# Order of the weight-form and tap transfers in the first step of a convolution and feed-forward kernel

## The chip, the cores and the metric

The kernel runs on one core of a Trainium2 chip. The metric is device time in microseconds, from a few timed runs of the whole program; lower is better. The trace comes from one more execution under the hardware profiler. Its span runs from the first to the last instruction of the program.

The engines are named as in the profile: PE (matrix products; PEld is its weight load), DVE (vector), ACT (scalar activation), POOL (general purpose; it also issues DMAs with accumulation), SP (issues DMAs). Each engine works through its own instructions in order. Transfers issued by POOL go to DMA queue q0, those by SP to q1; both run on the same 16 DMA engines.

## The reference

The input x is 8 x 4096 x 192. A causal convolution over 7 positions comes first, whose 7 weights (a softmax per head, 8 heads of 24 columns) are shared by the columns of a head. The result goes through a feed-forward block with 2048 hidden columns and a sigmoid form of gelu:

```python
w = softmax(weight)                         # 8 heads x 7 taps
out[b, s, h, :] = sum(w[h, k] * x_pad[b, s + k, h, :] for k in range(7))
h = out.reshape(32768, 192) @ w_in          # 192 -> 2048
g = h * (1.0 / (1.0 + np.exp(-1.702 * h)))
y = g @ w_out                               # 2048 -> 192
```

## The kernel before, in words

**Steps.** The 32768 tokens are worked through in 32 steps (`big` 0 to 31 in the code), each of 512 positions of two batch entries. In each step the convolution yields blocks C11 to C32 (two by three blocks: 192 columns in three parts, c = 0, 1, 2), the first product (L614) yields the hidden columns, ACT applies gelu, and the second product (L989) yields the output. Both products use a scheme with fewer block products and more additions: V1 to V8 are sums of convolution blocks (`SUMS_C`, L159), of which V1 = C31 - C11 comes first, and 21 terms (`TERMS`, L206) make one of the two halves (v = 0, 1) of the first product. The second product needs sums of the output weights, the *weight forms* (25 of them, in `w_out_s` and `w_form`).

**Step 0 is special.** It uses plain products, because weights and sums are still being made: `first_step` (L1096) and, for its second product, the generator `second_first` (L763). Its second product is done by `go` (L817; lines L820 and L825 in the profile). Beside it run the preparation of step 1's and step 2's convolutions and the making of the weight forms.

**Weight forms.** `add_forms(stage)` (L430) makes a form by a copy on ACT (L433 or L435) and one or two accumulating transfers on POOL's queue (L437), in four stages. Stage 3 has four transfers, called F1 to F4 here: (23 += 0), (24 += 3), (1 += 22) and (7 += 21), 192 KB each. Afterwards `end_forms` (L439; L441 in the profile) negates forms 9, 17, 20 and 21 on ACT. Form 21 is read by F4, so its negation waits until F4 has landed. `end_forms` stands in the list `todo`, behind the preparation of step 2, and is reached in the second half (v = 1) of step 1's first product.

**Taps.** The convolution of a later step is made part by part. For c = 1, DVE multiplies and adds (L504). For c = 0 and 2, ACT multiplies x by each of the seven weights (`tap`, L512; L516 in the profile) and writes the product to a spare place, its home. For c = 0 the seven products are added by six accumulating transfers on POOL's queue (`TREE`, L509; L530 in the profile), 256 KB each. For step 2 they are called T1 to T6 here: T1 adds home 2 to home 1, T2 home 4 to 3, T3 home 6 to 5, T4 home 1 to the result, T5 home 5 to 3, T6 home 3 to the result. So T5 needs T2 and T3, and T6 needs T4 and T5. For c = 2, POOL itself adds each home to the result (L518), six additions. After these POOL makes V1 and the other sums (`sums_c`, L532; L393 and L391 in the profile). SP then copies V1 across the two halves of the partitions (`cross`, L539; L541 in the profile).

**What sets the order.** The order on each engine is that of the calls in the code, as no scheduler moves them. `ready` holds step 2's fourteen taps (c = 0, then c = 2); each `next_tap()` (L1052) issues one. In `second_first` nine of them are issued (L879 to L888), the others in `hidden` by `taps_at` (L669) in step 1. Transfers of a tree that are due are put in the list `tree`, and `end_taps(left)` (L527) issues them down to `left`. In step 2, `end_taps(2)` at the seventh tap of c = 0 leaves T5 and T6 in the list; the next tap, the first of c = 2, calls `end_taps(0)` and issues them. Only then does `first_step` call `add_forms(3)` (L1227), and then `end_taps()` (L1228) and the x load for step 3 (L1229).

**Where PE needs step 2.** In the second half of step 1's first product (`hidden`, L662, v = 1), PE does term 7, term 12, terms 5 and 17, then, once ACT has copied a bank (`copy2(k15, ...)`, L651 in the profile), term 0 and 13 more terms; then `fetch` (L1241) begins step 2's first product with term 16, which reads V1 and its copy across; then come terms 3 and 19.

Of the kernel before, what the change touches and what calls it, by code (L numbers as in the profile page):

```python
# [15 lines left out]
def kernel(  # L16
# [32 lines left out]
    H, K = weight.shape  # L49
# [126 lines left out]
    def own(big):  # L176
        return conv_t[:, big % 2 * 2, :, :]
# [41 lines left out]
    def form(i):  # L219

        if i < WHOLE:
            return w_out_s[:, i // NG, i % NG * NG : (i % NG + 1) * NG, :]
        return w_form[:, i - WHOLE, :, :]
# [206 lines left out]
    def add_forms(stage):  # L430
        for dst, src, *sign in COPY_O[stage]:
            if sign:
                act.mul(form(dst), form(src), -1.0)  # L433
            else:
                act.copy(form(dst), form(src))  # L435
        for dst, src in SUMS_O[stage]:
            nc.gpsimd.dma_start(out=form(dst), in_=form(src), accum_op=ALU.add)  # L437
# [49 lines left out]
    def tap_home(big, c, k):  # L487
        if big == 1:
            return homes_1[c][k - 1]
        if big < 3:  # L490
            return (first_taps if c == 0 else taps[3])[k - 1]
        return taps[c][k - 1]

    def conv_src(big, c, k, ns=slice(0, 2)):
        return xts[big][:, c, ns, Q - PAD + k : Q - PAD + k + T]

    def conv(big, c, k, ns=slice(0, 2), times=vec.tensor_scalar_mul):
        src = conv_src(big, c, k, ns)
        dst = own(big)[:, 2 * c + ns.start : 2 * c + ns.stop, :]
        tap = cw[:, c, k : k + 1]  # L500
        if k == 0:
            times(dst, src, tap)
        else:
            vec.scalar_tensor_tensor(  # L504
                out=dst, in0=src, scalar=tap, in1=dst, op0=ALU.mult, op1=ALU.add
            )
# [5 lines left out]
    def tap(big, c, k):  # L512

        dst = own(big)[:, 2 * c : 2 * c + 2, :]
        home = tap_home(big, c, k) if k else dst
        act.mul(home, conv_src(big, c, k), cw[:, c, k : k + 1])  # L516
        if k and c not in DMA_TAPS and big > 1:
            nc.gpsimd.tensor_add(dst, dst, home)  # L518
            return
        homes = [dst] + [tap_home(big, c, i) for i in range(1, K)]  # L520
        for a, b in (PAIRS_1 if big == 1 and c == 0 else TREE).get(k, ()):
            tree.append((homes[a], homes[b]))
        end_taps(2 if big == 2 and k == K - 1 else 0)

    tree = []

    def end_taps(left=0):  # L527
        while len(tree) > left:
            out, src = tree.pop(0)
            nc.gpsimd.dma_start(out=out, in_=src, accum_op=ALU.add)  # L530
# [71 lines left out]
    def prepare_taps(big):  # L602

        for c in (0, 2):
            for k in range(K):
                yield "", 1.0, lambda c=c, k=k: tap(big, c, k)
        yield f"taps {big}", 0.0, lambda: None
# [155 lines left out]
    def second_first(between, fetch, last_taps):  # L763
# [53 lines left out]
        def go(bank, steps, first=True, more=False):  # L817
            for i, (w, t) in enumerate(steps):
                for c in range(NC):
                    nc.tensor.matmul(  # L820
                        chunk(bank, c), w[:, chunk_cols(c)], t,
                        start=first and i == 0, stop=not more and i == len(steps) - 1, skip_group_check=True,
                    )
                dst, w, t, start, to = side.pop(0)
                nc.tensor.matmul(dst, w, t, start=start, stop=to is not False, skip_group_check=True)  # L825
                if to is not False:
                    act.copy(to, dst)
# [17 lines left out]
            (listed(s1, t1, (0,)), None, True), (listed(s1, t1, (1,)), p5, False), (p3[:6], q12, False),  # L845
        )
        last_taps()
        sub(t1[1], b12[1], b11[1])
        add(s1[1], a21[1], a22[1])
        go(a, listed(a11, b11))  # L850
# [1 line left out]
        sub(t2[1], b22[1], t1[1])  # L852
        for i in range(2):
            sub(s2[i], s1[i], a11[i])
        add_forms(0)
        need("first 1")
        go(c11, p2[:6], more=True)
        add_forms(1)
# [23 lines left out]
        for i in range(0, len(steps), 2):  # L882
            go(c21, steps[i : i + 2], first=False)
            if i in (0, 2):
                act.copy(sums[i // 2], slots[2][i // 2])
            next_tap()
            if i < 6:
                next_tap()  # L888
        assert not side
        turn(0, 0, blocks(p1), js)  # L890
# [161 lines left out]
    def next_tap():  # L1052
        if ready:
            ready.pop(0)[2]()
            while ready and ready[0][1] == 0:
                ready.pop(0)[2]()

    def need(label):
        for q in (todo, ready):
            while any(item[0] == label for item in q):  # L1060
                q.pop(0)[2]()
# [34 lines left out]
    def first_step(fetch):  # L1096
# [99 lines left out]
        def between():  # L1196
# [4 lines left out]
            ready.extend(prepare_taps(2))  # L1201

        rest = second_first(between, fetch, lambda: taps_next(len(taps_1)))

        def stage(n, todo=lambda: next(rest)):
# [88 lines left out]
```

## Time and profile before

| What | us |
|---|---|
| timed runs, median of three | 2286.95 |
| timed runs, lowest and highest | 2285.14, 2287.42 |
| the profiled execution's own time | 2284.85 |
| its span | 2282.9 |
| ACT busy | 1563.2 |
| POOL busy | 847.4 |

The profile's times count from the start of the span. A row of the timeline gives the start, the length, engine, line, operation and shape, how many instructions were merged, and in brackets how long the engine stood idle before and what ended that. A row of the chain of work gives start, length and what the time was spent on; "DMA a<-b" is a transfer from its issue to its landing. The granted clock is the share of its full speed that PE's clock was allowed.

### The profile page before, as it was taken

The page shows a single profiled execution, that of the slowest core. Times are in us where ns is not written, and L with a number is a line of the kernel's source. Part 1 is how long each engine was busy: PE and PEld are TensorE (multiplying, and loading weights), DVE is VectorE, ACT ScalarE, POOL GpSimd, SP SyncE. Part 2 cuts the span into 40 slices and gives each one's busy share as a digit, 9 for nine tenths or more (in the row PEclk, how much of TensorE's full clock was granted, in tenths as well). Part 3 has the DMA queues.
Part 4 walks back from the last instruction along what each step waited for, and adds up shares of the span by engine and source line. Part 5 has one row for each costly group of instructions (what it writes and reads, how often), then busy time and mean ns, then how long its engine had stood idle before and what let it go on. Part 6 is the DMA issues. An engine that isn't in the chain of part 4 may idle for free.

```text
span 2282.9 us, 60959 instructions
## 1 busy us (share of the span) xinstructions
PE 2266.0 (99%) x25214; PEld 1202.3 (53%) x25214; DVE 1934.6 (85%) x2794; ACT 1563.2 (68%) x2968; POOL 847.4 (37%) x834
## 2 busy tenths in 40 slices
PE   9989999999999999999999999999999999999999
PEld 4355555555555555555555555555555555555556
DVE  8878888888888888888888888888888888888877
ACT  8657766667766677666776667776667766667754
POOL 1444442343433444324434234443244442344400
PEclk9999999999999999999999999999999999999999
DMA  9966566575666665665656666556756566574443
GB/s 205 165 133 135 114 127 129 122 142 109 117 126 139 127 126 112 128 134 123 137 115 120 126 130 136 118 111 124 143 121 135 112 128 130 123 141 84 91 98 71
DMA packets 270228, 285.78 MB, mean 125 GB/s; under 512 B 118016, under 2 KB 206080, under 8 KB 269824
## 3 DMA queue, kind: packets, MB, share of 16 engines
q0 software_dynamic: 57648, 150.69, 36.8%
q1 hardware_dynamic: 210656, 130.80, 25.6%
q8 instruction: 199, 3.26, 0.6%
q14 instruction: 77, 0.63, 0.1%
q10 hardware_dynamic: 1648, 0.39, 0.1%
HBM read 53.15 MB, written 25.17 MB: 34 GB/s over the span
## 4 chain that ended last, share of the span: by engine, by line
PE 94%; DVE 2%; DMA 2%; ACT 1%; issue 0%; POOL 0%; SPq 0%; DVEq 0%; POOLq 0%; ACTq 0%
PE slot L614 33%; PE slot L989 33%; PE sums L614 15%; PE sums L989 12%; DMA g<-g 1%; DMA w_form<-w_form 0%; DMA conv_t<-conv_t 0%; DVE xt L473 0%; DMA w_out_s<-w_form 0%; DVE g L832 0%; DVE conv_t L504 0%; DVE w_in_s L391 0%; DMA xin<-in_x_dram 0%; DVE w_in_s L393 0%; DVE w_out_s L376 0%
## 5 line engine op out<-in xcount | busy, mean ns | idle before, releaser
L614 PE MATMUL slot<-conv_t,w_in_s 64*128 64x512 f32 x3740 | 862.1, 592 | 8.9 <-ACT room L651 8.6
L989 PE MATMUL slot<-g,w_form 128*32 128x256 f32 x7024 | 710.3, 379 | 0.0
L614 PEld LDWEIGHTS slot<-conv_t,w_in_s 64*128 64x128 f32 x3740 | 374.8, 187 | 435.7 <-issue 352.4
L393 DVE TENSOR_TENSOR g<-g 128x1024 f32<-128x1024 f32 x372 | 448.1, 1232 | 4.1 <-ACT g L640 0.8
L989 PEld LDWEIGHTS slot<-g,w_form 128*32 128x32 f32 x7024 | 373.5, 110 | 119.7
L614 PE MATMUL sums<-conv_t,w_in_s 64*128 64x512 f32 x1660 | 408.5, 591 | 0.3 <-DVE w_in_s L376 0.3
L640 ACT ACTIVATE g<-room 128x1024 f32<-128x1024 f32 x310 | 325.8, 1077 | 68.1 <-DVE room L655 66.3
L1014 ACT COPY room<-slot 32x256 f32<-32x256 f32 x434 | 159.2, 367 | 310.4 <-PE slot L989 309.3
L989 PE MATMUL sums<-g,w_form 128*32 128x256 f32 x2648 | 368.8, 379 | 0.0
L989 PE MATMUL slot<-g,w_out_s 128*32 128x256 f32 x4080 | 318.8, 380 | 0.0
L965 POOL DMA_DIRECT2D g<-g x124 | 106.3, 857 | 502.5 <-PE slot L989 157.3
L614 PEld LDWEIGHTS sums<-conv_t,w_in_s 64*128 64x128 f32 x1660 | 172.0, 187 | 187.8 <-issue 142.6
L518 POOL TENSOR_TENSOR conv_t<-conv_t,g 128x512 f32<-128x512 f32 x180 | 260.6, 1448 | 15.6 <-POOL conv_t L518 3.3
L530 POOL DMA_DIRECT2D g<-g x120 | 104.7, 890 | 424.4 <-PE sums L989 128.7
L651 ACT COPY room<-slot 128x512 f32<-128x512 f32 x434 | 231.5, 601 | 41.4 <-PE slot L614 41.4
L516 ACT ACTIVATE g<-xt,cw 128x512 f32<-128x512 f32 x360 | 248.5, 730 | 2.2
L989 PEld LDWEIGHTS slot<-g,w_out_s 128*32 128x32 f32 x4080 | 164.7, 110 | 131.7 <-ACT g L636 22.7
L636 ACT ACTIVATE g<-slot 128x512 f32<-128x512 f32 x334 | 180.8, 598 | 45.2 <-PE slot L614 25.1
L989 PEld LDWEIGHTS sums<-g,w_form 128*32 128x32 f32 x2648 | 177.9, 110 | 36.7
L504 DVE SCALAR_TENSOR_TENSOR conv_t<-xt,cw,conv_t 128x512 f32<-128x512 f32 (+1 forms) x198 | 187.9, 949 | 4.6
L393 POOL TENSOR_TENSOR conv_t<-conv_t 128x256 f32<-128x256 f32 x180 | 185.7, 1046 | 9.4
L1014 ACT COPY room<-sums 32x256 f32<-32x256 f32 x217 | 79.6, 367 | 144.2 <-PE sums L989 142.5
(204 smaller groups left out, 2899.0 us busy)
## 6 DMA issues: line engine op xcount, KB each, us to landing
g<-g POOLq DMA_DIRECT2D x124, 512.0 KB, 5.6
xin<-in_x_dram SPq DMA_DIRECT2D x240, 180.0 KB, 4.4
conv_t<-conv_t SPq DMA_DIRECT2D x180, 192.0 KB, 3.2
g<-g POOLq DMA_DIRECT2D x120, 256.0 KB, 3.7
out_dram<-osbs SPq DMA_DIRECT2D x186, 128.0 KB, 4.9
g<-room POOLq DMA_DIRECT2D x31, 512.0 KB, 5.3
conv_t<-g POOLq DMA_DIRECT2D x60, 256.0 KB, 4.7
g<-osbs POOLq DMA_DIRECT2D x30, 512.0 KB, 4.6
```

Source lines behind the costliest of these rows:

```text
L393: eng.tensor_sub(v(dst), v(a), v(b))
L504: vec.scalar_tensor_tensor(out=dst, in0=src, scalar=tap, in1=dst, op0=ALU.mult, op1=ALU.add)
L516: act.mul(home, conv_src(big, c, k), cw[:, c, k : k + 1])
L518: nc.gpsimd.tensor_add(dst, dst, home)
L530: nc.gpsimd.dma_start(out=out, in_=src, accum_op=ALU.add)
L614: nc.tensor.matmul(slot[h], w_in_s[halves[h], a, v * P : (v + 1) * P], src, start=first, stop=True, skip_group_check=True,)
L636: act.activation(dst[:, :, h, :], src[h].rearrange("p (o t) -> p o t", o=2), AF.Gelu_apprx_sigmoid)
L640: act.activation(dst.rearrange("p o h t -> p h o t"), src.rearrange("p h (o t) -> p h o t", o=2), AF.Gelu_apprx_sigmoid,)
L651: act.copy(bank(dst, h), bank(src, h))
L965: nc.gpsimd.dma_start(out=spot(dst), in_=spot(a), accum_op=ALU.add)
L989: nc.tensor.matmul(dst, w, t, start=first, stop=last, skip_group_check=True)
L1014: act.copy(to, d)
```

## The change

Three places are edited. `end_taps` leaves two transfers in the list at every tap of step 2's part c = 2 too (and at the last of c = 0), so T5 and T6 are issued by the `end_taps()` behind `add_forms(3)`. `second_first` issues eight of step 2's taps instead of nine; the ninth goes to the next place in `hidden` that takes a tap, and each later tap moves on by one. `add_forms(0)`, the first eight form copies on ACT with their six transfers on POOL, stands ahead of the first product `go(a, listed(a11, b11))` and so ahead of the copy `act.copy(p1, whole(a))` on ACT.

```diff
@@ tap
-        end_taps(2 if big == 2 and k == K - 1 else 0)
+        end_taps(2 if big == 2 and (c or k == K - 1) else 0)
@@ second_first
         last_taps()
+        add_forms(0)
         sub(t1[1], b12[1], b11[1])
         add(s1[1], a21[1], a22[1])
         go(a, listed(a11, b11))
         act.copy(p1, whole(a))
         sub(t2[1], b22[1], t1[1])
         for i in range(2):
             sub(s2[i], s1[i], a11[i])
-        add_forms(0)
         need("first 1")
@@ second_first, last loop
             next_tap()
-            if i < 6:
+            if i < 4:
                 next_tap()
```

On each engine this gives: PE, DVE and SP keep their order (on DVE only line numbers differ). On ACT the eight copies (L433, L435) come ahead of the product's copy (L851 before), and the taps shift as told. On POOL, T5 and T6 (L530) come behind F1 to F4 (L437), and all six additions of c = 2 (L518) follow T6; before, the first of the six stood between T6 and F1.

## The prediction

> **What bounds the kernel now.** I read the page first, then the waits of PE over the whole span, then the chain of work that ended last around the one long wait, then that stretch window by window.
>
> ```profile
> span 2282.9 us, 60959 instructions
> PE 2266.0 (99%) x25214; PEld 1202.3 (53%) x25214; DVE 1934.6 (85%) x2794; ACT 1563.2 (68%) x2968; POOL 847.4 (37%) x834
> PE slot L614 <- ACT room L651: 8.6, 1, 8.6
> ```
>
> PE is busy 2266.0 of 2282.9 us, so all its idle time is 16.9 us, and one single wait of 8.6 us holds half of it. The profiled execution took 2284.85 us: its span and 1.95 us around it. The three timed runs have a median of 2286.95, 2.1 us above it; I work out a difference on the profiled execution and apply it to the median. No edit touches steps 3 to 31, so all that can change lies around that wait. The chain there:
>
> ```profile
> 107.28 6.97 DMA g<-g
> ...
> 118.42 5.38 DMA w_out_s<-w_form
> ...
> 123.88 0.52 ACT w_form L441
> ...
> 124.93 2.56 PE slot L614 x4
> ```
>
> Read upwards: PE restarts at 124.93 because ACT copies its bank only then; ACT stands in end_forms (L441), which may negate form 21 only when the last form transfer, F4, has landed, at 118.42 + 5.38 = 123.80; F4 was issued late because POOL, which issues in order, stood before tap transfer T6 until T5 had landed, at 107.28 + 6.97 = 114.25. The wait began at 124.93 - 8.6 = 116.3. The clock adds to it (columns: window, length, busy times, then granted clock, DMA share, GB/s):
>
> ```profile
> 118.00:120.00 2.00, 0.00 (x0) 0.00 (x0) 0.00 (x0) 0.00 (x0) 2.00 (x5) 1.00 0.92 142
> 120.00:122.00 2.00, 0.00 (x0) 0.00 (x0) 0.00 (x0) 0.00 (x0) 2.00 (x2) 0.58 1.11 178
> ...
> 130.00:132.00 2.00, 2.00 (x11) 1.70 (x9) 0.33 (x1) 0.56 (x2) 1.92 (x3) 0.86 0.29 70
> ```
>
> A mean of 0.58 over 120 to 122 is a clock that falls to one half at 120.3, 4 us into the wait; 0.86 over 130 to 132 is one that is whole again at 130.56. From 124.93 on PE thus works 5.6 us at half speed, a loss of 2.8. So the wait costs 8.6 + 2.8 = 11.4 us, and that is all this change can reach.
>
> **Edit 1: T5 and T6 behind F1 to F4.** POOL's queue before, and behind it SP's first cross transfers:
>
> ```profile
> 95.62 3.98 POOL L530 DMA_DIRECT2D g<-g  x3
> 101.66 1.19 POOL L530 DMA_DIRECT2D conv_t<-g  x1 [2.06 <-PE sums L614]
> 107.28 1.19 POOL L530 DMA_DIRECT2D g<-g  x1 [4.43 <-DMA g<-g]
> 114.78 1.19 POOL L530 DMA_DIRECT2D conv_t<-g  x1 [6.32 <-PE slot L614]
> 115.53 1.74 POOL L518 TENSOR_TENSOR conv_t<-conv_t,g 128x512 f32<-128x512 f32 x1
> 116.74 2.28 POOL L437 DMA_DIRECT2D w_form<-w_out_s  x2
> ...
> 118.99 8.46 POOL L518 TENSOR_TENSOR conv_t<-conv_t,g 128x512 f32<-128x512 f32 x5
> 127.53 3.38 POOL L393 TENSOR_TENSOR conv_t<-conv_t 128x256 f32<-128x256 f32 x2
> 129.15 1.11 SPq L541 DMA_DIRECT2D conv_t<-conv_t  x2
> conv_t<-conv_t SPq DMA_DIRECT2D x2, 64.0 KB, 2.0
> ```
>
> Rows one to four are T1 to T3, T4, T5, T6. After the edit the order is T1 to T4, F1 to F4, T5, T6, then six L518 additions. F1 to F4 wait for their ACT copies (four of 0.43 to 0.5 us behind the tap at 94.22 that edit 2 shows, so done by 97) and for landed sums, so POOL issues them from about 102.2, right behind T4, in place of 116.7. That is 14 us earlier, but not landed 14 us earlier, since the transfers are bound by the DMA engines (rows: queue, packets, MB, share of the 16 engines; windows 104:108, 110.3:123.8 and 118:124), and the x loads for step 3 stand in SP's queue just then:
>
> ```profile
> q0 software_dynamic: 415, 0.41, 69.3%
> q1 hardware_dynamic: 1149, 0.28, 40.9%
> ...
> q0 software_dynamic: 1084, 1.27, 62.0%
> q1 hardware_dynamic: 1970, 1.19, 47.6%
> ...
> q0 software_dynamic: 676, 0.87, 91.9%
> 103.61 8.81 SPq L99 DMA_DIRECT2D xin<-in_x_dram  x8
> ```
>
> T4 landed at about 110.3 (the ACT row below waits for it until 110.40). From there to 123.80 the engines moved T5, T6 and F1 to F4 (1.27 MB) and the x loads (1.19 MB) with shares of together 109%: 13.5 us without a hole worth naming. With POOL's queue alone it is 0.87 MB in 5.8 us, 0.15 MB/us. The same work is left after the edit; only the order changes. F1 to F4 are 4 x 192 KB = 0.79 MB, T5 0.26 MB.
> - Bound from above: all x loads are served first, and only T6's 0.26 MB are left: 0.26 / 0.15 = 1.7 us. T5 lands at 123.8 - 1.7 = 122.1 and F4 1.7 ahead of it, at 120.4.
> - Bound from below: POOL's queue gets 69.3 of 110.2 parts, 63%, as in 104:108. F4 lands 0.79 / 0.15 / 0.63 = 8.4 us after 110.3, at 118.7, T5 0.26 / 0.15 / 0.63 = 2.8 later, at 121.5. At 0.18 MB/us (the 0.36 MB that the queue moved in 120:122, its fullest window) these are 117.3 and 119.6.
>
> I take about the middle: **F4 at 118.8, T5 at 121.0**. PE restarts 1.13 us after F4 (124.93 - 123.80), at 119.9 in place of 124.93: 5.0 us won, and the wait is then 3.6 us.
>
> What is late next: T6, the six additions (L518), V1 = C31 - C11 (the first L393) and its cross over SP (L541) all stand behind T5 on POOL. PE needs V1 when fetch begins step 2's first product. In the trace:
>
> ```profile
> 138.97 3.59 PE L614 MATMUL slot<-conv_t,w_in_s 64*128 64x512 f32 x15
> 186.40 9.03 POOL L518 TENSOR_TENSOR conv_t<-conv_t,g 128x512 f32<-128x512 f32 x6
> 195.51 0.73 POOL L393 TENSOR_TENSOR conv_t<-conv_t 128x256 f32<-128x256 f32 x1
> ```
>
> The first row gives 0.86 us for the four matmuls of a term (15 in 3.59, the last one 0.59 long). Its first four are term 18, so fetch began at 138.97 + 0.86 = 139.83: 14 terms (12.0) and the 2.8 of slow clock after the restart. V1 was ready at 129.15 + 0.5 + 2.0 = 131.7 (the second SP cross goes out 0.5 after the first, and the last row of POOL's fence has 2.0 to landing): 8 us early. After the edit it is T5's landing, 0.53 to T6's issue (114.78 - 114.25), 0.75 to the first addition (115.53 - 114.78), the six additions, V1, and 2.6 for the cross. The additions: 9.03, as step 3's six (second row), beside a busy DVE. V1: 0.73 there, 1.6 in 127.53's row (two in 3.38); I take 1.1. Sum 14.0. **V1 is ready at 121.0 + 14.0 = 135.0**; PE, on a clock that has not fallen, comes to fetch at 119.9 + 12.0 = 131.9 and waits 3.1 us. Fetch begins at 135.0 in place of 139.83: **4.8 us won**, not 11.4. With the ends of T5 (119.6, 122.1) and of the tail (13.6, 14.5) it is 133.2 to 136.6, a gain of 3.2 to 6.6.
>
> This sum hardly depends on the first wait's clock. If the clock does fall there, PE comes to fetch 2.8 later, at 134.7, still ahead of V1. The Trainium skill, in "TensorE: Matmul & The Clock Gate", section "Part 1: The HAM clock gate", says that a whole idle window of about 3.4 us halves the clock, that the windows run freely, and that one busy window restores it. The trace agrees as far as it goes: half speed about 4 us into the wait. By that rule either new wait can fall on a whole window or miss it.
>
> **Edit 2: one tap fewer in step 0.** The ACT rows:
>
> ```profile
> 94.22 0.72 ACT L516 ACTIVATE g<-xt,cw 128x512 f32<-128x512 f32 x1
> ...
> 110.40 1.06 ACT L640 ACTIVATE g<-room 128x1024 f32<-128x1024 f32 x1 [1.78 <-DMA conv_t<-g]
> ...
> 123.88 0.52 ACT L441 ACTIVATE w_form<-w_form 128x384 f32<-128x384 f32 x1 [8.26 <-DMA w_out_s<-w_form]
> ```
>
> The tap at 94.22 leaves, so the copies of F1 to F4 end 0.63 earlier; POOL reaches them only at 102.2, so that is worth nothing. Every later tap of step 2 slides one place, and the last lands between two L640, in the 1.78 us in which ACT waits for T4. Cost: nothing; without that cover 0.72 on ACT, ahead of a wait that ends later anyway. I take 0, bounds -0.6 and +0.7.
>
> **Edit 3: first form copies ahead of the first product's copy.**
>
> ```profile
> 62.81 0.58 ACT L851 COPY conv_t<-slot 96x512 f32<-96x512 f32 x1 [2.88 <-PE slot L820]
> 63.29 2.58 ACT L435 COPY w_form<-w_out_s 128x384 f32<-128x384 f32 x6
> 64.09 5.88 POOL L437 DMA_DIRECT2D w_form<-w_out_s  x6
> 62.78 6.34 DMA conv_t<-conv_t
> 70.57 0.86 POOL L437 DMA_DIRECT2D w_form<-w_form  x1 [0.59 <-DMA w_form<-w_out_s]
> 71.16 0.60 PE L820 MATMUL slot<-osbs,conv_t 128*32 128x512 f32 x3
> 94.07 0.86 POOL L437 DMA_DIRECT2D w_form<-w_form  x1 [12.48 <-DMA w_form<-w_form]
> ```
>
> The eight copies (six and two L433, 3.4 us) fill ACT's 2.88 us of waiting, and the copy of the product moves from 62.81 to about 63.5. PE uses that bank again only at 71.16: 7 us of cover. POOL may issue the first form transfer about 0.8 us earlier, but the tap transfers of step 1 ahead of it land only at 62.78 + 6.34 = 69.12, so it lands at about 70.3 as before, and every later form transfer waits for such landings, up to the 12.48 us wait at 94.07. Worth 0; bounds -0.8 (all of the earlier issue comes through) and +0.7 (the later copy).
>
> **Sum:** -4.8 + 0 + 0 = -4.8. The profiled execution gives 2284.85 - 4.8 = 2280.05, the median 2286.95 - 4.8 = **2282.1 us**. The bounds of all edits, -3.2 + 0.7 and -6.6 - 0.8, give 2279.5 to 2284.5 for this case alone.
>
> **The rivals.**
> 1. *The whole wait goes.* F4 lands by 115.6, where ACT would otherwise reach it, and V1 keeps its old place ahead of fetch: 2286.95 - 11.4 = 2275.6. Against it: the engines have work for 13.5 us after 110.3, and POOL's order puts V1 behind T5.
> 2. *The new wait at fetch halves the clock.* It is 3.1 us in my sum, and a clock that falls costs 2.8 afterwards: 2282.1 + 2.8 = 2284.9. For it: the wait is near the 4 us at which the clock fell; the clock page's rule, above, makes it a matter of phase.
> 3. *The tap chain eats the gain.* T5 lands where F4 did, at 123.8, because the larger backlog slows the engines: V1 at 137.8, a gain of 2.0; with additions of 1.6 us each, as slow as the first L393, it is 138.5, a gain of 1.3, and a clock fallen in the longer wait turns it into a loss of 1.5: 2285 to 2288.5, in the middle 2286.5.
> 4. *Slower: POOL's additions lose their quiet place.* Before, most of them ran while DVE stood idle (no DVE work from 118 to 122, in the windows above). Now they lie beside DVE's 1.23 us additions. If each of the six waits for one, the six take 9.03 + 6 x 1.23 = 16.4, V1 is ready at 142.4, PE has waited 8 us or more and the clock is down: 142.4 + 2.8 - 139.83 = 5.4 lost, 2292.3. It decides from the point where V1 comes after 139.83, that is, 4.8 later than in my sum. Against it: step 3's six took 9.03 beside DVE.
>    The Trainium skill, in "SBUF — State Buffer", section "SBUF: two separate sides", has a rule that speaks for it: VectorE and GpSimd share one port pair, held for a whole instruction, and the other blocks. The 9.03 shows far less than such a block for each of the six.
>
> DVE's 1.23 us is this row's length (two-input, 128x1024):
>
> ```profile
> 129.10 1.23 DVE L393 TENSOR_TENSOR osbs<-osbs,g 128x1024 f32<-128x1024 f32 x1 [0.57 <-ACT g L640]
> ```
>
> **How the numbers follow.** A difference under about 0.2% (4.6 us) cannot be told from no change in a measurement of this kernel. My forecast sits close to that bound, so its chance is split. Forecast 0.57, of which 0.37 lie beyond 0.2% and 0.20 within; rival 1 and its neighbours 0.10, faster; rival 2 0.10, within; rival 3 0.15, within; rival 4 0.08, slower. Faster 0.47, same 0.45, slower 0.08. The range takes in the forecast's own bounds and rivals 2 and 3 and leaves out 1, 4 and the slow end of 3: 2279.0 to 2287.0.
>
> **What would show it.** In the changed profile: PE's waits hold no 8.6; in its place are two, one of about 3.6 that ACT ends (L651, behind L441) near 119.9 and one of about 3.1 that a conv_t transfer of SP ends near 135. POOL's L437 stand right behind the conv_t<-g at 101.7; T5 lands near 121; six L518 follow T6 and end near 131.5; the last L614 of step 1 ends about 4.8 us ahead of the old 138.97 + 3.59 = 142.6. The clock over 120 to 132 stays at or near 1.00. The forecast is wrong if F4 lands before 116 or after 121, if the second wait is missing, or if it is over 5 us.

## The result and the profile after

| | runs | median us | lowest to highest |
|---|---|---|---|
| before | 13 | 2285.31 | 2282.53 to 2288.49 |
| changed | 13 | 2281.64 | 2279.28 to 2283.73 |

The ratio is 0.9981, with a 95% interval of 0.9972 to 0.9989: about 4 us (2.5 to 6.4) faster. That is small, but the interval stays clear of 1. The profiled execution took 2281.64 us. First the top of its page:

```profile
span 2279.6 us, 60958 instructions
PE 2268.2 (100%) x25214; PEld 1198.7 (53%) x25214; DVE 1942.0 (85%) x2794; ACT 1563.4 (69%) x2968; POOL 849.1 (37%) x834
```

The span is 3.3 us shorter than before (2282.9). PE's idle time fell from 16.9 to 11.4, by 5.5, but its busy time rose by 2.2 for the same 25214 matmuls. In the stretch told below PE worked 6.8 us at half clock, where it worked 5.6 before; that makes 0.6 of the 2.2, and the rest was not traced. PE's waits (total, times, longest):

```profile
PE slot L614 <- DMA conv_t<-conv_t: 2.6, 1, 2.6
PE slot L614 <- ACT room L651: 1.6, 1, 1.6
```

The one wait of 8.6 became two. The chain of work that ended last (start, length) says what each hangs on:

```profile
105.10 11.73 DMA w_out_s<-w_form
...
116.91 0.52 ACT w_form L441
117.43 0.48 ACT room L651
...
117.96 1.12 PE slot L614 x2
...
131.63 0.74 POOL conv_t L393
...
132.90 2.00 DMA conv_t<-conv_t
134.90 0.14 issue
135.03 4.47 PE slot L614 x12
```

F4 landed at 105.10 + 11.73 = 116.83 (before 123.80), ACT negated form 21, and PE restarted at 117.96. Then V1 and its cross over SP end the chain: landed at 134.90, fetch at 135.03 (before 139.83). POOL's timeline shows the new order, T4, F1 to F4, T5, T6, six additions, V1:

```profile
102.73 1.19 POOL L530 DMA_DIRECT2D conv_t<-g  x1 [2.55 <-PE slot L614]
103.46 2.27 POOL L437 DMA_DIRECT2D w_form<-w_out_s  x2
104.56 2.94 POOL L437 DMA_DIRECT2D w_out_s<-w_form  x2
108.18 1.20 POOL L530 DMA_DIRECT2D g<-g  x1 [0.69 <-DMA g<-g]
119.70 1.19 POOL L530 DMA_DIRECT2D conv_t<-g  x1 [10.32 <-DMA g<-g]
120.45 11.10 POOL L518 TENSOR_TENSOR conv_t<-conv_t,g 128x512 f32<-128x512 f32 x6
```

POOL now stands idle for 10.32 us before T6, with the six additions behind it. Last, windows of 2 us (behind the window and its length come the engines' busy times, PE's first; third from the end is the granted clock):

```profile
118.00:120.00 2.00, 2.00 (x7) 1.24 (x9) 1.07 (x2) 2.00 (x5) 0.30 (x1) 0.81 1.18 243
120.00:122.00 2.00, 2.00 (x6) 0.89 (x4) 2.00 (x2) 1.37 (x2) 2.00 (x2) 0.50 0.92 184
122.00:124.00 2.00, 2.00 (x10) 1.18 (x8) 1.90 (x2) 0.61 (x2) 1.92 (x2) 0.84 0.71 100
...
136.00:138.00 2.00, 2.00 (x8) 1.45 (x6) 0.72 (x1) 0.00 (x0) 1.92 (x2) 0.57 1.12 239
138.00:140.00 2.00, 2.00 (x12) 0.32 (x12) 0.71 (x2) 0.00 (x0) 1.48 (x3) 0.57 1.13 220
```

The clock was at one half from 119.2 to 122.6 and from 136.3 to 139.7, 3.4 us each, behind both short waits. The first costs nothing, as PE still came to fetch ahead of V1. The second costs time: the twelve matmuls behind fetch took 4.47, where 2.73 lay between fetch and the end of the last L614 before (142.56 - 139.83). So 4.8 us were won at fetch, 1.7 given back to the clock, and 3.1 are left, the span's 3.3.

### The profile page after: what moved, and what is told of

Read it like the earlier page. It is cut to its first block, busy times and chain, and to the rows that moved or that the text cites. A ratio compares the mean times of both kernels' runs of the same rounds, so it can differ in the third digit from the quotient of the medians.

```text
span 2279.6 us, 60958 instructions
## 1 busy us (share of the span) xinstructions
PE 2268.2 (100%) x25214; PEld 1198.7 (53%) x25214; DVE 1942.0 (85%) x2794; ACT 1563.4 (69%) x2968; POOL 849.1 (37%) x834
## 4 chain that ended last, share of the span: by engine, by line
PE 98%; DMA 1%; ACT 0%; DVE 0%; POOL 0%; issue 0%; SPq 0%; DVEq 0%; ACTq 0%; POOLq 0%
PE slot L614 35%; PE slot L989 34%; PE sums L614 15%; PE sums L989 12%; PE slot L820 2%; DMA w_out_s<-w_form 1%; DMA xin<-in_x_dram 0%; POOL conv_t L518 0%; ACT conv_t L1094 0%; DVE xt L473 0%; DMA conv_t<-conv_t 0%; DVE conv_t L504 0%; SPq L99 0%; ACT conv_t L357 0%; ACT conv_t L356 0%
## 5 line engine op out<-in xcount | busy, mean ns | idle before, releaser
L614 PE MATMUL slot<-conv_t,w_in_s 64*128 64x512 f32 x3740 | 864.9, 592 | 4.5 <-DMA conv_t<-conv_t 2.6
L614 PEld LDWEIGHTS slot<-conv_t,w_in_s 64*128 64x128 f32 x3740 | 373.2, 187 | 435.3 <-issue 356.8
L393 DVE TENSOR_TENSOR g<-g 128x1024 f32<-128x1024 f32 x372 | 449.1, 1235 | 4.5 <-ACT g L640 1.3
L614 PE MATMUL sums<-conv_t,w_in_s 64*128 64x512 f32 x1660 | 409.4, 591 | 0.3 <-DVE w_in_s L376 0.3
L640 ACT ACTIVATE g<-room 128x1024 f32<-128x1024 f32 x310 | 325.8, 1077 | 72.1 <-DVE room L655 70.2
L614 PEld LDWEIGHTS sums<-conv_t,w_in_s 64*128 64x128 f32 x1660 | 171.4, 187 | 186.9 <-issue 140.8
L518 POOL TENSOR_TENSOR conv_t<-conv_t,g 128x512 f32<-128x512 f32 x180 | 261.6, 1453 | 14.1 <-POOL conv_t L518 2.6
L530 POOL DMA_DIRECT2D g<-g x120 | 104.7, 890 | 421.3 <-PE sums L989 128.7
L651 ACT COPY room<-slot 128x512 f32<-128x512 f32 x434 | 231.5, 601 | 40.3 <-PE slot L614 40.3
L636 ACT ACTIVATE g<-slot 128x512 f32<-128x512 f32 x334 | 180.8, 598 | 45.1 <-PE slot L614 24.6
L504 DVE SCALAR_TENSOR_TENSOR conv_t<-xt,cw,conv_t 128x512 f32<-128x512 f32 (+1 forms) x198 | 190.7, 963 | 4.6
L393 POOL TENSOR_TENSOR conv_t<-conv_t 128x256 f32<-128x256 f32 x180 | 186.8, 1051 | 9.4
```

The source lines that it names most:

```text
L393: eng.tensor_sub(v(dst), v(a), v(b))
L504: vec.scalar_tensor_tensor(out=dst, in0=src, scalar=tap, in1=dst, op0=ALU.mult, op1=ALU.add)
L614: nc.tensor.matmul(slot[h], w_in_s[halves[h], a, v * P : (v + 1) * P], src, start=first, stop=True, skip_group_check=True,)
L636: act.activation(dst[:, :, h, :], src[h].rearrange("p (o t) -> p o t", o=2), AF.Gelu_apprx_sigmoid)
L640: act.activation(dst.rearrange("p o h t -> p h o t"), src.rearrange("p h (o t) -> p h o t", o=2), AF.Gelu_apprx_sigmoid,)
L651: act.copy(bank(dst, h), bank(src, h))
```

## The experiments

The theory: the 8.6 us wait and its clock cost some 11.4 us; edit 1 removes most of the wait, and puts the chain T5, T6, additions, V1 in its place at fetch. Rivals: edits 2 or 3 do part of it; the x loads set when transfers land; SP's queue and not POOL's order ends the wait at fetch.

**Edit 1 alone** (e1_edit1_alone): before with the edited `end_taps` line.

> Edit 1 alone: T5 and T6 stand behind F1 to F4; the ninth tap and the place of the first form copies are as before. Theory (the gain is F4 landing ahead of T5 and T6, and it ends at V1): PE's 8.6 us wait falls under 3 us and a second wait appears at fetch. With nine taps issued early, the first of the six additions stands between T4 and F1, so only five stand behind T6; the second wait should be about 1.5 to 2 us shorter than the 2.6 of the changed kernel, and the time 1 to 2 us below the changed kernel's 2281.6: about 2280. Rival (the earlier form copies and the tap fewer are what brings the form transfers forward): F4 lands at 119 or later and the time stays within 1.5 us of the kernel before, near 2284 to 2285.

Measured: 2279.78 us (11 runs), ratio to before 0.9973 (0.9964 to 0.9982). POOL, then PE at fetch:

```profile
102.20 1.75 POOL L518 TENSOR_TENSOR conv_t<-conv_t,g 128x512 f32<-128x512 f32 x1
...
117.65 1.19 POOL L530 DMA_DIRECT2D conv_t<-g  x1 [8.85 <-ACT g L636]
118.41 9.74 POOL L518 TENSOR_TENSOR conv_t<-conv_t,g 128x512 f32<-128x512 f32 x5
```

```profile
131.63 1.77 PE L614 MATMUL slot<-conv_t,w_in_s 64*128 64x512 f32 x3 [2.37 <-DMA conv_t<-conv_t]
```

Edit 1 alone brings all of the gain. With nine taps issued in step 0, one addition still runs ahead of F1, and only five stand behind T6: from T6's issue to fetch it is 13.98 us, against 15.33 in the changed kernel (119.70 to 135.03). The wait at fetch was 2.4 us, where the expectation had 0.6 to 1.1: no wait was left ahead of it, so PE came to fetch earlier too.

**Edits 2 and 3 without edit 1** (e2_edits_2_and_3): the changed kernel with the old `end_taps` line.

> Edits 2 and 3 without edit 1: T5 and T6 ahead of F1 to F4 as before. Theory: no gain from the earlier copies; PE keeps one wait of 7.5 to 8.6 us that ACT ends behind L441, because F1 to F4 still follow T6. The only help is that no addition stands between T6 and F1 any more, which brings F1 forward by about 1 us: 2284 to 2285.3. Rival (edits 2 and 3 carry a good part of the gain): the wait falls under 6 us and the time under 2283.

Measured: 2285.34 us (11 runs), ratio 1.0 (0.9991 to 1.0009). In PE's waits the long one stands as before:

```profile
PE slot L614 <- ACT room L651: 8.9, 1, 8.9
```

Edits 2 and 3 bring nothing by themselves.

**Edits 1 and 3** (e7_edits_1_and_3), the changed kernel with nine taps in step 0, beside **the changed kernel again** (after_again) on the same chip.

```diff
-            if i < 4:
+            if i < 6:
```

> Edits 1 and 3 without edit 2 (nine taps in step 0). Theory (edit 2 is what costs 1 to 2 us of edit 1's gain, as it puts the first of the six additions behind T6): the first addition stands between T4 and F1 again, five follow T6, V1 is ready about 1.5 earlier than in the changed kernel, and the time is that of edit 1 alone, 2279.8, within 1. Rival (edit 3 costs it, by bringing the first forms' transfers forward into the x loads, or by the later copy): the time is that of the changed kernel, 2281.6 within 1, and the two waits of 1.6 and 2.6 us stand as there.

> The changed kernel once more, beside the three others on the same chip: 2281.6 within 1, two waits of about 1.6 and 2.6 us and half clock for one window of 3.4 us behind each. If a wait of under 3 us drops the clock only by the phase of a window, one of the two half-clock stretches can be missing here, and the time is then up to 1.7 us less.

Measured: 2279.78 us (7 runs), ratio 0.9974 (0.9963 to 0.9985), and 2281.16 us (11 runs), ratio 0.998 (0.9971 to 0.9989). POOL and PE with edits 1 and 3 (an execution that was later as a whole, with T4 landed at 112.94 and two more waits of PE, 2.0 for a gelu and 1.0 for L651):

```profile
121.03 1.19 POOL L530 DMA_DIRECT2D conv_t<-g  x1 [8.52 <-ACT g L636]
121.78 9.76 POOL L518 TENSOR_TENSOR conv_t<-conv_t,g 128x512 f32<-128x512 f32 x5
```

```profile
135.02 1.09 PE L614 MATMUL slot<-conv_t,w_in_s 64*128 64x512 f32 x3 [2.37 <-DMA conv_t<-conv_t]
```

and of the changed kernel again:

```profile
117.88 1.19 POOL L530 DMA_DIRECT2D conv_t<-g  x1 [10.58 <-DMA g<-g]
118.63 11.11 POOL L518 TENSOR_TENSOR conv_t<-conv_t,g 128x512 f32<-128x512 f32 x6
```

```profile
133.30 1.39 PE L614 MATMUL slot<-conv_t,w_in_s 64*128 64x512 f32 x4 [3.62 <-DVE g L391]
```

From T6's issue to fetch: 13.99 and 15.42. With the first pair, 13.98 and 15.33: whatever the starting time, edit 2 puts one more addition on this path and costs 1.4 us there. (Where T6's row names ACT's L636, T5 had landed 0.3 before the issue, at 117.37 and 120.74, as in the changed kernel at 119.41, so I read it as T5's landing.) The medians say the same (1.4 apart), though their intervals overlap. Edit 3 cost nothing that shows. The second profile of the changed kernel also shows how much one execution says: its first wait was 0.3 us, not 1.6, its fetch wait 3.6, not 2.6, and only one half-clock stretch came. Its fetch releaser is named as DVE's L391, which ended at 133.24; the cross of V1 landed at 133.16, and PE started 0.14 after that, as in the other profiles, so I read it as the cross.

**Half of the x loads** (e6_half_the_x_loads): the changed kernel with `load_x(3, (0,))` for `load_x(3)`, which leaves one of the two batch entries of step 3 unloaded; one profile.

> The changed kernel with half of the x load for step 3 left out (only one of its two batch entries is loaded, so step 3 works on old data in the other half). Theory (F1 to F4 and T5 are bound by the DMA engines, which they share with the x loads): F4 lands 1 to 2 us earlier than 116.8 and T5 1.5 to 2.5 earlier than 119.4, the 1.6 us wait behind F4 goes or is nearly gone, and the one at fetch shrinks by about what T5 gains. Rival (they are bound by their own queue or by their order, one behind the other): F4 within 0.4 of 116.8 and T5 within 0.4 of 119.4.

The theory is not borne out. This execution (2283.55 us) was later as a whole (T4 issued at 105.34, not 102.73), so lengths are compared: T4's landing to F4's 5.2 us (113.90 to 119.11), between the changed kernel's two profiles with all x loads, 6.4 and 4.8 (109.81 to 114.61); F4 to T5 2.2 against 2.6 and 3.0. The other seven profiles with F1 to F4 ahead of T5, all x loads in place, have 5.2 to 6.3 and 2.0 to 2.5. Queue shares (queue, packets, MB, share of the 16 engines) from T4's landing to F4's, of the changed kernel:

```profile
q0 software_dynamic: 715, 0.88, 82.0%
q1 hardware_dynamic: 844, 0.47, 32.2%
```

and with half of the x loads:

```profile
q0 software_dynamic: 581, 0.70, 78.7%
q1 hardware_dynamic: 759, 0.46, 36.8%
```

POOL's queue gets about 80% in both (89.9% in the changed kernel's second profile, 109.8 to 114.6). The x loads give way, and themselves land later (the last at 124.0, before at 118.9). Halving them saves nothing that stands out from the spread between profiles, for F4 or for T5; as this is one profile, a saving under 1 us is not excluded.

**Negation late** (e4_negation_late): the kernel before, with `end_forms` moved further back on ACT, behind the gelu of `k15` in step 1's second half. ACT reaches it at 128.76, when F4 has landed (123.60), so no PE work waits for F4.

```diff
@@ hidden
-        taps_at(2)
+        end_forms() if v and big == 1 else taps_at(2)
@@ first_step
-            todo.append(("forms", 0.0, end_forms))
```

> The kernel before with one thing moved: ACT negates the four forms (L441) 14 instructions later, behind the second L640 of the half, where F4 has landed. POOL, SP, DVE and PE keep their order. Theory (PE's 8.6 us are ACT standing at L441 for F4, and nothing else): the wait vanishes though F4 lands as late as before. PE reaches fetch at 116.3 + 12.0 = 128.3, V1 is ready at 131.7 as before, so a wait of about 3.4 us stands at fetch; 8.1 us are won there, less 0 to 3 for a clock that falls: 2277 to 2280. Rival (the DMA engines are the bound of this stretch, whatever ACT does): the wait turns up elsewhere in the same stretch with 6 us or more, time 2283 or above.

Measured: 2281.04 us (11 runs), ratio 0.998 (0.9971 to 0.9988). PE's waits:

```profile
PE slot L614 <- DMA conv_t<-conv_t: 3.0, 1, 3.0
PE slot L614 <- ACT g L636: 0.6, 1, 0.6
```

The 8.6 us wait goes without any transfer moved, and a wait for V1's cross at fetch, as in the changed kernel, appears in its place (132.60). The miss of 1 us comes with slower additions: five in 10.61 where before they took 8.46.

**Only T6 behind the additions** (e3_t6_behind_additions, e3_again): the changed kernel, in which the six additions need no longer wait for T5.

```diff
@@ tap, after the addition on POOL
-            return
+            return end_taps() if big == 2 and k == K - 1 else None
@@ first_step, behind add_forms(3)
-        end_taps()
+        end_taps(1)
```

> The changed kernel with one more move: T6 alone goes behind the six additions of c = 2, so the additions follow T5's issue and need not wait for T5's landing. Theory (the wait at fetch comes from the chain T5 landed, T6 issued, six additions, V1, cross): the additions start near 109 in place of 120.4, V1 is ready well ahead of 132.4, and the 2.6 us wait at fetch is gone with the half clock behind it (1.7 us lost). The first wait, 1.6 us behind F4, stays, and its half clock of one window of 3.4 us as well. That gives 2281.6 - 2.6 - 1.7 = 2277.3, expected 2276.5 to 2278. Rival (what ends the wait at fetch is the transfer queue, by SP's cross behind the x loads, whatever POOL does): the wait stays near 2.6 and the time within 1 of the changed kernel, 2280.6 to 2282.6.

> T6 behind the additions once more, beside the kernel that has the late negation too. Theory (with V1 early, the first wait is the only one left, and it lies between 0.3 and 1.6 us from one execution to the next): 2274.8 within 1, and 0.3 to 1.6 above the kernel with both. If its half clock comes in most executions, it is 2 to 3.3 above.

Measured: 2274.76 us (5 runs), ratio 0.9954 (0.9942 to 0.9967), and again 2275.79, ratio 0.996 (0.9948 to 0.9973). POOL of the first:

```profile
109.52 10.02 POOL L518 TENSOR_TENSOR conv_t<-conv_t,g 128x512 f32<-128x512 f32 x6
120.11 1.20 POOL L530 DMA_DIRECT2D conv_t<-g  x1 [0.58 <-DMA g<-g]
124.07 1.52 POOL L393 TENSOR_TENSOR conv_t<-conv_t 128x256 f32<-128x256 f32 x2 [2.75 <-DMA conv_t<-g]
```

The additions fill POOL's idle 10 us, V1 comes at 124.07, and the wait at fetch is gone: POOL's order was the cause, not the queue to SP. The median was 2.5 us below the forecast, which took the first wait and its half clock for fixed. In neither profile does PE wait for L651; each has an earlier wait, of 1.7 and 2.8 us, for a gelu of ACT (L636), with a half-clock stretch behind it. Both profiled executions were the slowest of their five, so that most runs probably lack it.

**Both** (e5_additions_before_t6_and_negation_late, e5_again): the two edits above, together, on the changed kernel.

> The changed kernel with two more moves: the six additions stand between T5 and T6 on POOL, so POOL does them while T5 is under way (it stood idle 10.3 us there), and ACT negates the forms 14 instructions later. Theory: the first wait goes altogether; the additions end near 120, T6 goes out near 120 and lands near 125, V1 is ready near 129 with its cross, PE comes to fetch at 128.4: a wait of 0 to 1 us. Against the kernel before 10.5 to 11.4 us are won: 2274 to 2275. Rival (something else in this stretch, such as the additions 3 to 5 holding up ACT's gelu, or the x loads, keeps the gain at the changed kernel's level): 2279 or above.

> T6 behind the additions and the late negation, once more: 2273.9 within 1, no wait of PE left between 100 and 140 us and the clock whole, 11.4 to 12 us less than the kernel before.

Measured: 2273.91 us (5 runs), ratio 0.9949 (0.9937 to 0.9962), 12.0 under its before (2285.94), and again 2274.84, ratio 0.9952 (0.9938 to 0.9966). The window 100 to 140 of the first run:

```profile
100.00:140.00 40.00, 40.00 (x308) 25.70 (x307) 35.72 (x44) 31.35 (x56) 26.17 (x23) 1.00 0.99 190
```

PE busy for 40.00 of 40 us at full clock. In the repeat one wait was left, which I had not expected:

```profile
PE slot L614 <- ACT g L636: 2.7, 1, 2.7
```

T4 landed there at 113.67, not 110.52, and ACT's L640, which waits for it ahead of that gelu, came late. T4's landing varied from 109.5 to 113.9 over the profiles; why wasn't tried. Beside each other on one chip, T6 behind the additions gave 2275.79 and both edits 2274.84: not to be told apart. Both beat the kernel before and the changed one.

**The changed kernel with the negation late** (e8_changed_and_negation_late).

> The changed kernel with the negation of the four forms moved behind the last gelu of that half, so that the wait behind F4 is gone by construction. Theory (PE's two waits are in series: time won ahead of fetch is only waited out at fetch, since V1 hangs on T5's landing): the wait behind L651 is gone, the wait at fetch grows by what that one was (0.3 to 1.6 us and 1.7 where its half clock goes), and the time is that of the changed kernel within 1, 2280.2 to 2282.2. Rival (the first wait costs time of its own): 1.5 to 3 us faster, 2278 to 2279.5.

Measured: 2280.4 us (10 runs), ratio 0.9978 (0.9969 to 0.9987). PE's waits:

```profile
PE slot L614 <- DMA conv_t<-conv_t: 2.7, 1, 2.7
PE slot L614 <- ACT g L636: 1.2, 1, 1.2
```

The first wait is gone, and fetch stays where V1 puts it (133.02). The gelu wait of 1.2 is new: ACT stood idle for 4.11 us ahead of that gelu until an addition on POOL (L518) ended, so additions that come late hold up ACT as well. The time fits the theory, that the first wait is absorbed at fetch; the interval does not wholly exclude the rival.

## Why the prediction was right, point by point

The forecast of 2282.1 lies 0.5 above the median after. The mechanism was right, but three terms were off and partly cancel, and the median of three runs from which it started (2286.95) was 1.6 above that of 13 (2285.31). From the median of 13 the same sum gives 2280.5, which is 1.1 too low: the forecast gain was 4.8, the measured one 3.7. That the forecast came within 0.5 is in part luck. Its 0.2% as the least that can be told from no change was too wide for 13 runs of each kernel, whose interval is 0.09% to each side.

- **The wait costs 11.4 us in all.** Borne out: with T6 behind the additions and the late negation the kernel is 12.0 and 11.1 us faster, the first with no wait left in its profile. That is rival 1's figure, but the change did not bring it.
- **F4 at 118.8:** mis-sized; 116.83 and 114.61 in two profiles, the second ahead of the 116 that the forecast named as a sign of being wrong. So the first wait was 1.6 and 0.3 us, not 3.6. The share of 63% for POOL's queue was the wrong row: it got 82 and 90%. It came from 104 to 108, in which POOL stood before a landing; with F1 to F4 and T5 queued the x loads yield.
- **T5 at 121.0:** 119.41 and 117.59; the same term.
- **T5 to V1, 14.0:** mis-sized; 15.5. The additions took 11.10 where step 3's 9.03 had been taken (why stands at the end), V1 0.74 where 1.1.
- **Fetch at 135.0:** 135.03, by luck: T5 forecast 1.6 too late and the way to V1 1.5 too short cancel; in the second profile 133.30. PE came to it at 132.4 (forecast 131.9) and waited 2.6 (3.1).
- **The clock stays near 1.00:** wrong. It was 0.50 over 120 to 122, harmless as forecast, and again behind the second wait. So rival 2 came true in its mechanism, at 1.7 us and not 2.8, since one stretch of 3.4 us at half speed costs 1.7. The gain of 3.1 in the trace lies between the forecast's 4.8 and rival 2's 2.0. The rule that the prediction quotes from the Trainium skill, "TensorE: Matmul & The Clock Gate", section "Part 1: The HAM clock gate", that a whole idle window halves the clock, is contradicted: PE was idle for 1.56 us (116.40 to 117.96) of the 3.41 ahead of the first drop, and for 2.16 of the second.
- **Edit 2 at 0:** wrong by 1.4 us, as a share of the sum and not in its total. I priced the tap on ACT, and not that the list `ready` moves with it: with edit 1 but without edit 2 the first addition on POOL stands ahead of F1, with edit 2 behind T6. The sum had all six additions behind T6, so this price was in its 14.0, under edit 1. The cover of ACT's idle time was there.
- **Edit 3 at 0:** as far as the runs show.
- **Rival 3** (T5 at 123.8): no; T5 landed 1.6 to 3.4 ahead of the forecast. **Rival 4** (POOL blocked beside DVE, 16.4 us): in part, 11.1; V1 stayed ahead of 139.83.

## What to carry to other kernels

When a wait is removed, ask what the same queue delivers next, and where its consumer stands: here the gain was bounded by V1 at fetch, whether the first wait was shortened by the order of transfers or taken out by the late negation. An engine that waits 10 us for a landing with independent work queued behind should do that work first; here that one move was worth more (6.4 us against the changed kernel beside it) than the whole change (4.4 on that chip). A call taken out of one loop shifts every later entry of the list that it draws from, on all engines.

## What was not expected of the hardware

Short waits halve the clock, but not always. Two kernels with waits of 2.4 and 2.7 us kept it whole. Windows of edits 1 and 3 (waits 132.65 to 135.02):

```profile
132.00:134.00 2.00, 0.65 (x3) 0.00 (x0) 2.00 (x4) 0.38 (x1) 1.84 (x4) 1.00 0.14 33
134.00:136.00 2.00, 0.98 (x5) 0.77 (x7) 2.00 (x4) 2.00 (x4) 1.92 (x2) 1.00 0.59 158
136.00:138.00 2.00, 2.00 (x14) 1.01 (x14) 1.72 (x2) 0.59 (x1) 1.92 (x2) 1.00 1.09 228
```

and of T6 behind the additions, again (wait 112.56 to 115.38):

```profile
114.00:116.00 2.00, 0.62 (x3) 0.43 (x4) 2.00 (x3) 2.00 (x4) 1.92 (x2) 1.00 1.16 227
116.00:118.00 2.00, 2.00 (x9) 1.20 (x9) 0.28 (x2) 2.00 (x4) 1.84 (x3) 0.72 1.17 239
118.00:120.00 2.00, 2.00 (x7) 1.04 (x6) 1.79 (x1) 1.92 (x6) 1.92 (x2) 0.50 1.19 230
```

In the first the clock stays at 1.00; in the second it falls at 116.9, after the wait is over. The two drops of the changed kernel lie 17.07 us apart, five times 3.413, which fits a decision at fixed ticks 3.413 us apart on the idle time since the last.

The traces bear this out, as each keeps the times at which the granted clock changed, the drop after PE's last work included, and all the changes of one execution lie whole multiples of that apart: in the changed kernel 627 times 3.4133 us from 139.70 to 2279.86. Counted back from that last drop (2277.41 with edits 1 and 3, 2271.51 with both edits again), a tick falls inside each of the two waits that kept the clock: at 133.84, which cuts 132.65 to 135.02 into 1.19 and 1.18 us, and at 114.28, which cuts 112.67 to 115.37 into 1.6 and 1.1. So a wait cut in two by a tick can pass. How much idle time of one 3.41 us stretch is enough is known only roughly: 1.22 us (the 1.2 in the last experiment) did not lower the clock, 1.56 did in the changed kernel, and 1.6 with both edits again did not.

POOL's additions are slowed by some of DVE's operations only. Two of the six in the changed kernel, and then DVE beside all six:

```profile
126.70 1.27 POOL L518 TENSOR_TENSOR conv_t<-conv_t,g 128x512 f32<-128x512 f32 x1
...
128.05 2.14 POOL L518 TENSOR_TENSOR conv_t<-conv_t,g 128x512 f32<-128x512 f32 x1
```

```profile
120.13 3.15 DVE L393 TENSOR_TENSOR osbs<-g 128x1024 f32<-128x1024 f32 x1
123.39 2.10 DVE L393 TENSOR_TENSOR osbs<-osbs,g 128x1024 f32<-128x1024 f32 x1
...
126.61 1.27 DVE L655 TENSOR_TENSOR room<-slot,room 128x512 f32<-128x512 f32 x2
127.81 1.25 DVE L391 TENSOR_TENSOR osbs<-g 128x1024 f32<-128x1024 f32 x1
128.98 2.08 DVE L473 STREAM_TRANSPOSE xt<-xin 128x576 f32<-128x576 f32 x3
```

Beside L655, which reads a product's bank (`slot`), an addition took 1.27, as with DVE idle (1.26 with edits 2 and 3); the one that began during L391, whose operands are both of `g`, took 0.87 more. The Trainium skill, in "SBUF — State Buffer", section "SBUF: two separate sides", says that VectorE and GpSimd block each other where a VectorE operation has two SBUF inputs. The runs agree for L391 and L393, and show 0.87 a meeting where rival 4 took 1.23. They do not show a full block beside L504, which reads two tiles (`xt`, `conv_t`) that are no product's bank either: the additions there took 1.6, 0.33 more. DVE pays as well: its two L393 above took 3.15 and 2.10, where the row in the prediction has 1.23. Three of the six additions met one (2.14 each), and the first, behind a DMA issue, took 1.74, as it did with DVE idle (1.76 with edits 1 and 3). Before, four of the five behind F4's issue began while DVE was idle (to 125.90), and step 3's 9.03 lay beside L655, L504 and L473 only. So the length of an addition is read from what DVE does beside it, not from how busy DVE is.
